# An attention block with a token mixer: the second column pair's fill goes first, and the last token pair takes narrow products over three steps

## The chip, the cores and the metric

The kernel runs on one core of a Trainium2 chip. The metric is device time in microseconds (us) of one execution. Below, PE is the matrix engine (TensorE) and PEld its weight loads, DVE is VectorE, ACT is ScalarE, POOL is GpSimd, and SP is SyncE, which issues most of the transfers (DMA).

## The reference, cut to what matters

Two residual blocks follow each other, on x with 2048 tokens and 512 channels, in float32:

```
h  = x + A(layernorm(x))      # linear attention, 32 heads of 16, dual softmax features, then @ wo
h2 = h + B(layernorm(h))      # token mixing:
    u = gelu(einsum("bsd,sf->bdf", hn, w1) + b1)     # contracts the 2048 tokens, F = 1792
    y = einsum("bdf,fs->bds", u, w2) + b2            # back to 2048 tokens
```

A needs all tokens' keys and values before any token's query can be finished. B's first product contracts the tokens, so it can start on the first tokens of h while the later ones are still in the attention.

## The kernel before, in words

**Precision.** Each float32 matrix product is made of three passes on rounded parts: high times high, high times low, low times high (`mm3`, lines 63 to 67). For every operand ACT writes the rounded part (`hi`), and DVE or POOL subtracts it from the source (`lo`; `split`, lines 58 to 61).

**Stages.** The 2048 tokens are 16 tiles of 128 (NT = 16). First come keys, values and some of the queries. Then the attention loop (lines 646 to 698) runs NT + 3 iterations; iteration `it` works on several tiles at once, each at another step: queries' features scaled on POOL (`s_pq`, line 463, and `s_ez`, line 445), transposes on PE (`s_tr`, line 530, copied out by ACT in line 532 as `pht`), numerators on PE (`s_num`, line 549, on every second iteration), the output projection (`s_wo`), the residual on DVE (`s_h`, line 577), and the second layernorm: `s_moments` on ACT, `s_rstd` on POOL (lines 588 and 589, tiles `r` and `ve`), and `s_hn` (line 593 on ACT, then the split: line 60 on ACT, line 61 on POOL). The result of `s_hn` is `HN[t]`, named `hs` in the profile.

**Fills.** B's first product is done in seven column pairs p of 256 columns of w1; each pair has two PSUM banks, `PU[p]` (named `pu`). `fill(p)` adds the share of one token tile to pair p: two `mm3`, so six matmuls of 128x512, shown at lines 65 to 67. In the attention loop `fills(it)` (lines 640 to 644) adds one tile to pair 0 and one to pair 1: pair 0 takes tile `it - 5`, pair 1 is a tile behind and takes tile `it - 6`. What is left of the pairs 0 and 1, and the pairs 2 to 6, runs after the loop, in an order that a scheduler makes. Weights come by DMA (line 611, `wraw`), ACT makes `whi` (line 612), DVE makes `wlo` (line 604). Within the attention loop the order on PE, DVE, ACT and POOL is that of the program text.

**Second product.** The outputs are made for pairs of token tiles, `sp` = 0 to 7. The two halves of F and the two tiles of a pair form a 2 by 2 block product, done by a scheme with seven products in place of eight, for each of seven steps p (`STEPS`, line 764). ACT and DVE prepare w2's sums in groups of two steps (`sums_w2`, `hi_w2` in line 793, `lo_w2` in line 802). The low parts live in two buffers, so a group's low part is written once the products of the group two before it are done.

**Wide and narrow products** (`product`, lines 818 to 825). A bank holds two halves of 256 columns. A wide product multiplies the high weights with both parts of `u` at once, 512 columns (line 820): high times high goes to half 0, high times low to half 1; then low times high, 256 columns, is added to half 0 (line 821). The two halves must be added on DVE later. A narrow product is three matmuls of 256 columns into one half (line 824), and needs no adding. In `PROD`, five of the seven products are wide; in `LAST`, for the last token pair, four are wide.

**Order at a pair's end.** The steps p = 0 to 4 run step by step (all seven products of a step). The last two steps run by product: product 0 of steps 5 and 6, then product 1 of both, and so on (line 857), so that the banks are complete one after another. For the last token pair the tail (lines 891 to 912) adds banks to the residual on DVE and writes three pieces of the output: one of 256 KB and two of 128 KB, the last at line 912.

Of the kernel before, what the change touches and what calls it, by code (L numbers as in the profile page):

```python
# [17 lines left out]
P = 128  # L18
S, D, H, DH, F = 2048, 512, 32, 16, 1792
NT = S // P  # L20
KD = D // P
NF = F // P
NP = NF // 2
HD = D // 2
# [6 lines left out]
LAG = 5  # L31
# [5 lines left out]
def block_kernel(ctx: ExitStack, tc: tile.TileContext, x, xT, wT, phic, wo, w1, b1, w2, b2,  # L37
                 kvmask, ident_in, out):
    nc = tc.nc
# [23 lines left out]
    def mm3(o, ah, al, bh, bl, first, last):  # L63

        nc.tensor.matmul(o, ah, bh, start=first, stop=False)  # L65
        nc.tensor.matmul(o, ah, bl, start=False, stop=False)  # L66
        nc.tensor.matmul(o, al, bh, start=False, stop=last)  # L67
# [3 lines left out]
    ps_q = ctx.enter_context(tc.tile_pool(name="ps_q", bufs=2, space=PSUM, side="right"))  # L71
# [290 lines left out]
    q = {"mm": 0, "logits": 0, "exp": 0, "sum": 0}  # L362
# [238 lines left out]
    def flush():  # L601
        while LATER:
            wl_, raw, wh_ = LATER.pop(0)
            LO.append(nc.vector.tensor_sub(wl_, raw, wh_).ins)  # L604
# [13 lines left out]
    FN, FL = [0] * (NF // 2), [0] * (NF // 2)  # L618

    def fill_load(p):  # L620
        if FL[p] < NT:
            WI[p, FL[p]] = stream(w1v, FL[p], 2, p * 256, 256)
            FL[p] += 2

    def fill(p, pool=None):

        t = FN[p]
        FN[p] = t + 1
        if FL[p] <= t:
            fill_load(p)  # L630
        if any(part is WI[p, t - t % 2][1] for part, _, _ in LATER):
            flush()
        if t == 0:
            PU[p] = [pool.tile([P, D], F32, name="pu", tag="pu") for _ in range(2)]
        a, b = WI[p, t - t % 2]
        for c in range(2):
            mm3(PU[p][c], a[:, t % 2, c * P:(c + 1) * P], b[:, t % 2, c * P:(c + 1) * P],
                HN[t][:, 0], HN[t][:, 1], t == 0, t == NT - 1)

    def fills(it):  # L640
        if FN[0] <= it - LAG:
            fill(0, ps_f)
        if FN[1] < it - LAG:
            fill(1, ps_q)

    for it in range(NT + 3):
        even = it % 2 == 0
# [23 lines left out]
        negate()  # L671
        q_mm()
        fills(it)
        q_exp(0)
        logits = q_logits(1)
# [110 lines left out]
    def hi_w2():  # L786

        g = done["hi"]
        if g == NGR:
            return  # L790
        done["hi"] += 1
        WH[g] = ws.tile([P, 7, GRP * P], F32R, name="whi", bufs=3)
        nc.scalar.activation(WH[g], RAW[g], AF.Copy)  # L793

    def lo_w2():

        g = done["lo"]
        if g == NGR:
            return
        done["lo"] += 1  # L800
        wl_ = ws.tile([P, 7, GRP * P], F32R, name="wlo", bufs=2)
        nc.vector.tensor_sub(wl_, RAW[g], WH[g])  # L802
        for i, step in enumerate(STEPS[g * GRP:(g + 1) * GRP]):
            AW[step] = WH[g][:, :, i * P:(i + 1) * P], wl_[:, :, i * P:(i + 1) * P]

    with tc.issue_after(LO[-18]), tc.issue_after(LD[-20]):
        for i in range(3):
# [5 lines left out]

    PROD = ((2, 1, 0, None), (5, 5, 1, None), (0, 0, 2, 0), (1, 4, 2, 1), (3, 6, 3, None), (6, 2, 4, None),
            (4, 3, 5, None))
    LAST = PROD[:-1] + ((4, 3, 5, 0),)

    def product(o, half, a, b, first, start, stop):
        if half is None:
            nc.tensor.matmul(o, a[0], b, start=start, stop=stop, skip_group_check=True)  # L820
            nc.tensor.matmul(o[:, 0], a[1], b[:, 0], start=False, stop=stop, skip_group_check=True)  # L821
            return
        for i, (x, y) in enumerate(((0, 0), (0, 1), (1, 0))):
            nc.tensor.matmul(o[:, half], a[x], b[:, y], start=start and first and i == 0, stop=stop and i == 2,  # L824
                             skip_group_check=True)

    def products(sp, ps, order):
        for a, b, bk, half in order:
            for p in ps:
                wh_, wl_ = AW[sp, p]  # L830
                product(bank[bk], half, (wh_[:, a], wl_[:, a]), UB[p, b], half != 1, p == 0, p == NP - 1)

    def flat(a):
        return a.rearrange("p k d -> p (k d)")
# [3 lines left out]
    for n, (sp, p) in enumerate(STEPS):  # L838
        t = 2 * sp
        last = t + 2 == NT  # L840
        if n % GRP == 0 and p < NP - 1:
            lo_w2()
            hi_w2()
            sums_w2()
        if p == 0:
            bank = []
            for _ in range(6):
                pool = (ps_f, ps_q, ps_b, ps_b)[n_bank % 8 // 2]
                bank.append(pool.tile([P, 2, HD], F32, name="py", tag="pu"))
                n_bank += 1  # L850
        order = LAST if last else PROD
        if p < NP - 2:
            products(sp, [p], order)
            continue
        if p < NP - 1:
            continue
        products(sp, [p - 1, p], order)
        e = uo.tile([P, 2, HD], F32, name="e")
        u2 = uo.tile([P, HD], F32, name="u2", bufs=1)
        u3 = uo.tile([P, HD], F32, name="u3")  # L860
        if not last:
            ot = uo.tile([P, 2, 2, HD], F32, name="ot", bufs=1)
            low = uo.tile([P, 3, HD], F32, name="low", bufs=1)
            nc.scalar.activation(e[:, 1], bank[0][:, 0], AF.Copy)
            for i in range(3):
                nc.scalar.activation(low[:, i], bank[3 + i][:, 1], AF.Copy)
            nc.vector.tensor_add(e[:, 1], bank[0][:, 1], e[:, 1])
            nc.vector.tensor_sub(u2, bank[1][:, 0], e[:, 1])
            nc.vector.tensor_add(u2, bank[1][:, 1], u2)
            nc.vector.tensor_sub(u3, u2, bank[2][:, 0])  # L870
            nc.vector.scalar_tensor_tensor(e[:, 0], bank[2][:, 1], -1.0, u2, op0=ALU.mult, op1=ALU.subtract)

            def out_block(i, h, o, add):
                nc.vector.scalar_tensor_tensor(ot[:, i, h], o, b2s[:, t + i:t + i + 1], add, op0=ALU.add, op1=ALU.add)  # L874

            out_block(0, 0, bank[2][:, 1], u3)
            out_block(0, 1, bank[3][:, 0], u3)
            nc.gpsimd.dma_start(out[t * P:(t + 1) * P, :], flat(ot[:, 0]), accum_op=ALU.add)  # L878
            if n % GRP == 0:
                lo_w2()  # L880
                hi_w2()
            out_block(1, 0, bank[4][:, 0], e[:, 0])
            out_block(1, 1, bank[5][:, 0], e[:, 1])
            nc.gpsimd.dma_start(out[(t + 1) * P:(t + 2) * P, :], flat(ot[:, 1]), accum_op=ALU.add)
            nc.gpsimd.dma_start(out[t * P:(t + 1) * P, HD:D], low[:, 0], accum_op=ALU.add)
            nc.gpsimd.dma_start(out[(t + 1) * P:(t + 2) * P, :], flat(low[:, 1:3]), accum_op=ALU.add)
            if n % GRP == 0:
                sums_w2()
            continue

        hb = [hp.tile([P, 2, HD], F32, name=f"hb{i}") for i in range(2)]
        for i in range(2):
            nc.sync.dma_start(flat(hb[i]), out[(t + i) * P:(t + i + 1) * P, :])
            nc.vector.tensor_scalar(hb[i], hb[i], b2s[:, t + i:t + i + 1], None, op0=ALU.add)
        nc.scalar.activation(e[:, 1], bank[0][:, 0], AF.Copy)
        nc.vector.tensor_add(e[:, 1], bank[0][:, 1], e[:, 1])
        nc.vector.tensor_add(hb[1][:, 1], e[:, 1], hb[1][:, 1])
        nc.vector.tensor_sub(u2, bank[1][:, 0], e[:, 1])
        nc.vector.tensor_add(u2, bank[1][:, 1], u2)
        nc.vector.tensor_sub(hb[1][:, 0], hb[1][:, 0], u2)  # L900
        nc.vector.tensor_sub(u3, u2, bank[2][:, 0])
        nc.vector.tensor_sub(hb[1][:, 0], hb[1][:, 0], bank[2][:, 1])
        nc.vector.tensor_add(hb[0], hb[0], u3.unsqueeze(1).to_broadcast([P, 2, HD]))
        nc.vector.tensor_add(hb[0][:, 0], bank[2][:, 1], hb[0][:, 0])
        nc.vector.tensor_add(hb[0][:, 1], bank[3][:, 0], hb[0][:, 1])
        nc.vector.tensor_add(hb[0][:, 1], bank[3][:, 1], hb[0][:, 1])
        nc.sync.dma_start(out[t * P:(t + 1) * P, :], flat(hb[0]))
        nc.vector.tensor_add(hb[1][:, 0], bank[4][:, 0], hb[1][:, 0])
        nc.vector.tensor_add(hb[1][:, 0], bank[4][:, 1], hb[1][:, 0])
        nc.scalar.dma_start(out[(t + 1) * P:NT * P, 0:HD], hb[1][:, 0])  # L910
        nc.vector.tensor_add(hb[1][:, 1], bank[5][:, 0], hb[1][:, 1])
        nc.sync.dma_start(out[(t + 1) * P:NT * P, HD:D], hb[1][:, 1])


def _layout(A_x, A_wqkv, A_w_phi, A_wo, B_w1, B_b1, B_w2, B_b2):
# [46 lines left out]
```

## Time and profile before

| | |
|---|---|
| median of 3 runs | 529.30 us (529.26 to 529.55) |
| the profiled execution | 529.31 us |
| its span, first to last instruction | 527.5 us |
| PE busy | 516.5 us (98%), 3343 matmuls |
| DVE, ACT, POOL busy | 394.5, 278.3, 246.6 us |
| granted PE clock, mean | 0.999 |

The span stands 1.8 us below the profiled execution's time; the rest lies around it. A PE matmul is shown as busy until its modelled end, and matmuls overlap, so busy time of PE hides short stops: these are read from the waits and from the distance of starts in the timeline. In a timeline row the first number is the start in us, the second the duration; "x8" is eight instructions merged in a row; in brackets stands how long the engine was idle before, and what ended the wait. The chain of waits goes back from the last instruction to what released it, and so on.

### The profile page before, as it was taken

Reading aid. Unit: us, or ns where it says so; the run is one execution under the profiler, and the core shown is the slowest. Engines: PE = TensorE matmul, PEld = TensorE weight load, DVE = VectorE, ACT = ScalarE, POOL = GpSimd, SP = SyncE. Lnnn points to the kernel's source line nnn. Section 1 sums busy time; section 2 is a strip of 40 time slices with the busy share of each in tenths; the row PEclk is TensorE's granted clock in tenths of the full one; section 3 lists DMA queues with packets and bytes.
Section 4 is the critical chain, followed back from the end, with each engine's and each line's share of the span. In section 5 each row is a group of like instructions: output and inputs, shape, how many; then the busy total and the mean of one; then the engine's idle time right before and its main releaser. Section 6 shows DMA issues by size and latency. Waiting matters only on the chain.

```text
span 527.5 us, 8840 instructions
## 1 busy us (share of the span) xinstructions
PE 516.5 (98%) x3343; PEld 434.1 (82%) x3343; DVE 394.5 (75%) x684; ACT 278.3 (53%) x481; POOL 246.6 (47%) x204
## 2 busy tenths in 40 slices
PE   8999999999999989999999999999999999999996
PEld 7888888887877767777788888888899999999995
DVE  6993999976899989875325523725779888988985
ACT  6999843534247776557746423625453434434430
POOL 2589699985999988887326000000002112111210
PEclk9999999999999999999999999999999999999999
DMA  8743310030122233334234354532215687668742
GB/s 298 203 129 121 84 39 21 1 86 18 49 93 80 91 96 115 109 111 139 85 99 119 99 161 155 166 98 80 69 51 113 160 187 169 135 146 198 141 61 60
DMA packets 36298, 58.52 MB, mean 111 GB/s; under 512 B 3744, under 2 KB 19360, under 8 KB 36256
## 3 DMA queue, kind: packets, MB, share of 16 engines
q1 hardware_dynamic: 31936, 51.37, 31.2%
q0 software_dynamic: 4032, 6.42, 9.6%
q8 instruction: 26, 0.43, 0.4%
q10 hardware_dynamic: 288, 0.17, 0.1%
q14 instruction: 16, 0.13, 0.1%
HBM read 46.81 MB, written 11.14 MB: 110 GB/s over the span
## 4 chain that ended last, share of the span: by engine, by line
PE 80%; POOL 12%; DVE 4%; ACT 2%; DMA 1%; issue 0%; DVEq 0%; POOLq 0%; ACTq 0%
PE py L820 12%; PE pu L65 11%; PE pu L66 10%; PE pu L67 10%; PE py L824 8%; PE py L821 6%; POOL ez L445 4%; POOL eq L463 3%; PE pv L66 3%; PE pv L67 3%; PE pv L65 3%; PE pk_ps L65 2%; PE pk_ps L67 2%; PE pk_ps L66 2%; POOL hs L61 2%; PE kvp L210 2%
## 5 line engine op out<-in xcount | busy, mean ns | idle before, releaser
L604 DVE TENSOR_TENSOR wlo<-wraw,whi 128x512 fp32r<-128x512 f32 x56 | 50.6, 908 | 54.6 <-ACT whi L612 53.4
L66 PE MATMUL pu<-hs,whi 128*128 128x512 f32 x224 | 87.6, 391 | 2.1 <-POOL hs L61 2.1
L65 PE MATMUL pu<-hs,whi 128*128 128x512 f32 x224 | 87.5, 395 | 0.0
L67 PE MATMUL pu<-hs,wlo 128*128 128x512 f32 x224 | 87.3, 390 | 0.0
L878 POOL DMA_DIRECT2D out<-ot x7 | 6.2, 889 | 149.1 <-DVE ot L874 149.1
L793 ACT ACTIVATE whi<-wraw 128x1792 fp32r<-128x1792 f32 x28 | 47.4, 1701 | 46.7 <-PE py L820 20.6
L820 PE MATMUL py<-uf,whi 128*128 128x512 f32 x195 | 70.9, 399 | 0.0
L802 DVE TENSOR_TENSOR wlo<-wraw,whi 128x1792 fp32r<-128x1792 f32 x28 | 56.5, 2022 | 12.0 <-PE py L821 8.9
L612 ACT ACTIVATE whi<-wraw 128x512 fp32r<-128x512 f32 x56 | 34.9, 626 | 47.3 <-PE pu L66 43.0
L821 PE MATMUL py<-uf,wlo 128*128 128x256 f32 x195 | 54.9, 282 | 0.0
L66 PEld LDWEIGHTS pu<-hs,whi 128*128 128x128 f32 x224 | 42.1, 188 | 11.5 <-POOL hs L61 3.1
L65 PEld LDWEIGHTS pu<-hs,whi 128*128 128x128 f32 x224 | 42.1, 188 | 10.8 <-issue 2.5
L67 PEld LDWEIGHTS pu<-hs,wlo 128*128 128x128 f32 x224 | 42.1, 188 | 9.0 <-DVE wlo L604 0.4
L820 PEld LDWEIGHTS py<-uf,whi 128*128 128x128 f32 x195 | 36.8, 189 | 7.3
L445 POOL TENSOR_TENSOR ez<-eq,zB 128x1024 f32<-128x1024 f32 x16 | 40.6, 2539 | 4.4 <-ACT zB L492 4.4
L821 PEld LDWEIGHTS py<-uf,wlo 128*128 128x128 f32 x195 | 36.9, 189 | 0.0
L198 POOL TENSOR_TENSOR pk<-pk,sk 128x1024 f32<-128x1024 f32 x16 | 31.0, 1943 | 7.9 <-DVE sk L197 5.3
L463 POOL TENSOR_TENSOR eq<-eq,w 128x1024 f32<-128x1024 f32 x16 | 31.9, 1997 | 1.2 <-DVE w L460 1.2
L824 PE MATMUL py<-uf,whi 128*128 128x256 f32 x170 | 32.0, 283 | 0.0
L202 POOL TENSOR_TENSOR zacc<-zacc,pk 128x1024 f32<-128x1024 f32 x13 | 31.2, 2402 | 0.5
L61 POOL TENSOR_TENSOR hs<-hn,hs 128x512 fp32r<-128x512 f32 x16 | 21.4, 1337 | 17.8 <-ACT hs L60 17.8
L820 PE MATMUL py<-un,whi 128*128 128x512 f32 x78 | 28.8, 399 | 0.0
(183 smaller groups left out, 1317.8 us busy)
## 6 DMA issues: line engine op xcount, KB each, us to landing
wraw<-in_w SPq DMA_DIRECT2D x56, 256.0 KB, 2.8
wraw<-in_w SPq DMA_DIRECT2D x28, 512.0 KB, 4.4
xraw<-in_xT SPq DMA_DIRECT2D x16, 256.0 KB, 2.9
xh<-in_x SPq DMA_DIRECT2D x16, 256.0 KB, 2.7
h<-in_x SPq DMA_DIRECT2D x16, 256.0 KB, 3.0
out<-h SPq DMA_DIRECT2D x16, 256.0 KB, 3.0
out<-ot POOLq DMA_DIRECT2D x14, 256.0 KB, 4.5
wraw<-in_wT SPq DMA_DIRECT2D x12, 256.0 KB, 5.2
```

The source lines that it names most:

```text
L65: nc.tensor.matmul(o, ah, bh, start=first, stop=False)
L66: nc.tensor.matmul(o, ah, bl, start=False, stop=False)
L67: nc.tensor.matmul(o, al, bh, start=False, stop=last)
L445: nc.gpsimd.tensor_mul(EZ[t], EQ[t], zB)
L463: nc.gpsimd.tensor_mul(heads(EQ[t]), heads(EQ[t]), W[t].rearrange("p g c h -> p (g c h)").unsqueeze(2).to_broadcast([P, 2 * H, DH]))
L604: LO.append(nc.vector.tensor_sub(wl_, raw, wh_).ins)
L612: nc.scalar.activation(wh_, raw, AF.Copy)
L793: nc.scalar.activation(WH[g], RAW[g], AF.Copy)
L802: nc.vector.tensor_sub(wl_, RAW[g], WH[g])
L820: nc.tensor.matmul(o, a[0], b, start=start, stop=stop, skip_group_check=True)
L821: nc.tensor.matmul(o[:, 0], a[1], b[:, 0], start=False, stop=stop, skip_group_check=True)
L824: nc.tensor.matmul(o[:, half], a[x], b[:, y], start=start and first and i == 0, stop=stop and i == 2, skip_group_check=True)
```

## The change

Two edits. In the attention loop, `fills` does pair 1 ahead of pair 0; no other order of the loop changes. For the last token pair, all seven products become narrow, so that four banks are used in place of six and the tail's additions of two halves go away (10 additions and subtractions on DVE in place of 14, the two of b2 counted in neither); and the last three steps (4, 5 and 6) run by product, in place of the last two.

```
     def fills(it):
+        if FN[1] < it - LAG:
+            fill(1, ps_q)
         if FN[0] <= it - LAG:
             fill(0, ps_f)
-        if FN[1] < it - LAG:
-            fill(1, ps_q)
...
-    LAST = PROD[:-1] + ((4, 3, 5, 0),)
+    LAST = ((2, 1, 0, 0), (5, 5, 0, 1), (0, 0, 1, 0), (1, 4, 1, 1), (3, 6, 2, 0), (6, 2, 2, 1), (4, 3, 3, 0))
...
-        if p < NP - 2:
+        run_on = 3 if last else 2
+        if p < NP - run_on:
             products(sp, [p], order)
             continue
         if p < NP - 1:
             continue
-        products(sp, [p - 1, p], order)
+        products(sp, range(NP - run_on, NP), order)
...
         nc.scalar.activation(e[:, 1], bank[0][:, 0], AF.Copy)
-        nc.vector.tensor_add(e[:, 1], bank[0][:, 1], e[:, 1])
-        nc.vector.tensor_add(hb[1][:, 1], e[:, 1], hb[1][:, 1])
-        nc.vector.tensor_sub(u2, bank[1][:, 0], e[:, 1])
-        nc.vector.tensor_add(u2, bank[1][:, 1], u2)
+        nc.vector.tensor_add(hb[1][:, 1], bank[0][:, 0], hb[1][:, 1])
+        nc.vector.tensor_sub(u2, bank[0][:, 1], e[:, 1])
         nc.vector.tensor_sub(hb[1][:, 0], hb[1][:, 0], u2)
-        nc.vector.tensor_sub(u3, u2, bank[2][:, 0])
-        nc.vector.tensor_sub(hb[1][:, 0], hb[1][:, 0], bank[2][:, 1])
+        nc.vector.tensor_sub(u3, u2, bank[1][:, 0])
         nc.vector.tensor_add(hb[0], hb[0], u3.unsqueeze(1).to_broadcast([P, 2, HD]))
-        nc.vector.tensor_add(hb[0][:, 0], bank[2][:, 1], hb[0][:, 0])
-        nc.vector.tensor_add(hb[0][:, 1], bank[3][:, 0], hb[0][:, 1])
-        nc.vector.tensor_add(hb[0][:, 1], bank[3][:, 1], hb[0][:, 1])
+        nc.vector.tensor_add(hb[0][:, 0], bank[1][:, 1], hb[0][:, 0])
+        nc.vector.tensor_sub(hb[1][:, 0], hb[1][:, 0], bank[1][:, 1])
+        nc.vector.tensor_add(hb[0][:, 1], bank[2][:, 0], hb[0][:, 1])
         nc.sync.dma_start(out[t * P:(t + 1) * P, :], flat(hb[0]))
-        nc.vector.tensor_add(hb[1][:, 0], bank[4][:, 0], hb[1][:, 0])
-        nc.vector.tensor_add(hb[1][:, 0], bank[4][:, 1], hb[1][:, 0])
-        nc.scalar.dma_start(out[(t + 1) * P:NT * P, 0:HD], hb[1][:, 0])
-        nc.vector.tensor_add(hb[1][:, 1], bank[5][:, 0], hb[1][:, 1])
-        nc.sync.dma_start(out[(t + 1) * P:NT * P, HD:D], hb[1][:, 1])
+        for k, o, q in ((0, bank[2][:, 1], nc.scalar), (1, bank[3][:, 0], nc.sync)):
+            nc.vector.tensor_add(hb[1][:, k], o, hb[1][:, k])
+            q.dma_start(out[(t + 1) * P:NT * P, k * HD:(k + 1) * HD], hb[1][:, k])
```

## The prediction

> **What bounds the kernel now.** I read the page's shares first, then busy time by stretch, then the waits, then the chain.
>
> ```profile
> span 527.5 us, 8840 instructions
> PE 80%; POOL 12%; DVE 4%; ACT 2%; DMA 1%; issue 0%; DVEq 0%; POOLq 0%; ACTq 0%
> ```
>
> The profiled execution took 529.31 us, 0.01 above the median of the runs, so 1.8 us lie around the span; the sum below is made against 529.31. Four fifths of the chain that ends last is PE. An eighth is POOL, and I want to know where that lies.
>
> ```profile
> 185.00:240.00 55.00, 51.12 (x358) 39.41 (x356) 47.54 (x87) 35.37 (x76) 48.08 (x37) 1.00 0.35 106
> 240.00:505.00 265.00, 265.00 (x1457) 228.50 (x1450) 174.60 (x285) 124.01 (x193) 45.27 (x52) 1.00 0.50 128
> ```
>
> The columns are PE, PEld, DVE, ACT, POOL busy, the clock, DMA. From 240 to 505 PE is never idle. From 185 to 240, the later part of the attention loop, it misses 3.9 us, and POOL works 48 of 55.
>
> ```profile
> ACT hn L593 <- POOL ve L589: 23.6, 13, 3.3
> ...
> POOL hs L61 <- ACT hs L60: 17.8, 10, 3.1
> ...
> PE pu L66 <- POOL hs L61: 2.1, 3, 1.0
> PE tn L549 <- ACT pht L532: 1.6, 2, 1.4
> ```
>
> These are whole waits in us, how often, and the longest. PE stops for two things: for `hs`, the layernormed tile that pair 0's fill needs (the first edit's target), and for `pht` ahead of `s_num`. Which of the two sets the end is read from the chain, here its last POOL piece:
>
> ```profile
> 229.31 1.89 POOL eq L463
> 231.21 1.23 POOL hs L61
> 232.43 2.81 POOL ez L445
> 235.24 0.51 POOL r L588
> 236.05 0.83 ACT hn L593
> 236.90 0.63 ACT hs L60
> 237.53 0.53 ACT whi L612
> 238.06 0.97 ACT pht L532 x2
> 239.08 1.10 PE tn L549 x32
> ```
>
> POOL's queue runs without a hole up to the reciprocal root `r` and `ve`; ACT, waiting for them, makes `hn` and `hs`, and behind these in its queue stands `pht`, for which PE's `s_num` waits. No PE instruction is in this chain. From 239.08 on it is PE, up to the tail.
>
> The tail, from the chain again:
>
> ```profile
> 518.55 0.39 ACT e L895
> 518.97 0.43 DVE e L896
> ...
> 521.44 0.33 DVE hb L902
> 521.77 0.61 DVE hb L903
> ```
>
> and as a timeline, then the last transfer in the view of DMA issues (its 1.7 us is from issue to landing):
>
> ```profile
> 518.23 0.28 PE L821 MATMUL py<-uf,wlo 128*128 128x256 f32 x1
> ...
> 522.51 0.28 PE L824 MATMUL py<-uf,wlo 128*128 128x256 f32 x1
> ...
> 524.33 0.41 DVE L911 TENSOR_TENSOR hb<-py,hb 128x256 f32<-128x256 f32 x1
> ...
> 524.77 0.34 SPq L912 DMA_DIRECT2D out<-hb  x1
> ```
>
> ```profile
> out<-hb SPq DMA_DIRECT2D x1, 128.0 KB, 1.7
> ```
>
> The last matmul ends at 522.51 + 0.28 = 522.79. DVE is in one unbroken run of 14 additions from 518.97 on and ends at 524.33 + 0.41 = 524.74, 1.95 us after PE. So here DVE is the bound.
>
> **First edit: pair 1's fill ahead of pair 0's.** It adds and removes nothing; six matmuls of 128x512 change places with six. Pair 1 uses a tile that is one iteration older, so its six can run while POOL makes `hs`. Stops for `hs`, 2.1 us by the waits, should go. What is late next is `s_num`: in the chain above it starts when `pht` is there, and that hangs on POOL and ACT alone. Each us that PE is earlier it waits more at line 549. The iterations before 185 have no such stop, and from 239.08 on PE has the same work to do. So I cost the edit at 0. The cover is POOL's chain; were it gone, up to 2.1 us would be gained, and this is the first rival. Can the block lose? Inside it, pair 1's operands must be ready 6 matmuls earlier; after it, everything stands where it stood on PE. No other engine's waits change in the built program: POOL, DVE and SP have the same order and wait for the same producers, and ACT has one `whi` behind instead of ahead of a short `ve` late in the loop, where the chain is PE's:
>
> ```profile
> 267.50 0.28 ACT L585 ACTIVATE ve<-ve,eps 128x1 f32<-128x1 f32 x1
> ```
>
> I take 0, since the chain is the nearest row; as bounds I keep -2.1 and, for that `ve` should its `whi` be wanted at once, +0.3.
>
> **Second edit, the matmuls.** Four wide products in each of seven steps become narrow: 28 times, two matmuls (512 and 256 columns) become three of 256. The columns streamed are the same 768. From the timeline:
>
> ```profile
> 503.05 0.41 PE L820 MATMUL py<-uf,whi 128*128 128x512 f32 x1
> ...
> 505.17 0.40 PE L820 MATMUL py<-un,whi 128*128 128x512 f32 x1
> ...
> 519.05 0.41 PE L824 MATMUL py<-uf,whi 128*128 128x256 f32 x2
> ...
> 520.49 0.40 PE L820 MATMUL py<-uf,whi 128*128 128x512 f32 x1
> ```
>
> Between the first two starts lie six wide products: 2.12 / 6 = 0.353 each. Between the other two, four narrow ones: 1.44 / 4 = 0.360. So PE's end moves by 28 x 0.007 = 0.2 us. This is the first term, +0.2.
>
> The Trainium skill, page "TensorE: Matmul & The Clock Gate", section "Back-to-back issue gap", lets a warm matmul of 256 columns take 262 cycles and one of 512 take 518, at 2.4 GHz. By it, an estimate, a narrow product takes 786 cycles and a wide one 780, 2.5 ns apart, so 28 of them make 0.07 us and the whole sum would be -1.4. The trace has longer spacings than that page for both, 0.360 and 0.353.
>
> **Second edit, the order.** Steps 4, 5 and 6 by product: 21 products of 0.36. Groups of three end 1.08 us apart. Readers in the built program wait for a whole bank. So bank 0 (products 0 and 1) is full 15 products before PE's end, 5.4 us; bank 1 3.2 us before; bank 2 1.1 us before; bank 3 at the end. The additions take 0.33 to 0.43 in the chain, the wide one 0.61:
> - after bank 0: ACT's copy 0.39 and three additions, 1.6 us with the steps between engines: done 3.8 before the end;
> - after bank 1: 0.6 + three of 0.4 = 1.8: done 1.4 before;
> - after bank 2: two, 0.8: done 0.3 before;
> - after bank 3: one, 0.42.
>
> DVE is never behind, so its end is PE's end + 0.04 (as from the bank's last matmul, ending 518.51, to the copy at 518.55) + 0.42 = PE's end + 0.46, in place of + 1.95. Second term: -1.49. The transfer behind it is the same 128 KB on the same queue, with the two others issued farther ahead of it; I leave its 1.7 and what follows as they are.
>
> One thing the new order needs earlier: the low weights of steps 5 and 6, by the third matmul of step 5's product 0.
>
> ```profile
> 512.93 2.02 DVE L802 TENSOR_TENSOR wlo<-wraw,whi 128x1792 fp32r<-128x1792 f32 x1 [1.64 <-PE py L824]
> 515.15 0.39 PE L820 MATMUL py<-uf,whi 128*128 128x512 f32 x1
> ```
>
> DVE makes them from 512.93 to 514.95, after PE has freed their buffer (end of step 2). Step 4 starts at 515.15; the third matmul of the second product comes 0.36 + 2 x 0.12 later, 515.75. That leaves 0.8 us; a wait here costs what it exceeds that.
>
> **Sum.** 0 + 0.2 - 1.49 = -1.3: 529.31 - 1.3 = 528.0 us, 0.25% less.
>
> **Rivals.**
> 1. *PE's stops for `hs` are on the path.* Then 2.1 us go too: 525.9 (the starts under rival 2 show 1.6 for the first stop, where the waits show 1.0, so it could be 3). For it: they are PE's only stops besides `pht`. Against: the chain above, and ACT's 23.6 us of waits for POOL's `ve`.
> 2. *One long stop lowers the clock.* The fills of the first stopped iteration, twelve matmuls from line 65 up to line 530, and the stop behind them:
>
> ```profile
> 185.39 0.47 PE L65 MATMUL pu<-hs,whi 128*128 128x512 f32 x1
> ...
> 189.79 1.03 PE L530 MATMUL tn<-ident,eq 128*128 128x128 f32 x8
> ...
> 194.98 0.45 PE L549 MATMUL tn<-pht,kvB 64*32 64x256 f32 x8 [1.42 <-ACT pht L532]
> ```
>
> ```profile
> 526.00:527.00 1.00, 0.00 (x0) 0.00 (x0) 0.00 (x0) 0.00 (x0) 0.00 (x0) 0.71 0.06 18
> ```
>
>    They take 4.40; at 0.353 for 768 columns (above), twelve of 512 would take 2.8. So PE comes 1.6 earlier to line 549 and stops for 1.42 + 1.6 = 3.0 us at a stretch. The second row is a stretch after PE's end: the clock is 0.71 in the mean of 526 to 527, so, if it went to half, it did so near 526.4, 3.6 us after the last matmul. Against: 3.0 is less than 3.6, though that is one sample. At half speed for as long as that, PE would lose 1.8; the other stops up to 239 (3.7 of all waits less the longest, 1.0 and 1.4) take 1.3 of it. Time: 528.0 + 0.5 = 528.5. The Trainium skill, same page, section "Part 1: The HAM clock gate (the "warmup" mystery)", has the clock halved after an idle window of about 3.4 us; 3.0 stays below that as well.
> 3. *Slower: narrow matmuls run at the pace of their weight loads.* Each has its own.
>
> ```profile
> L824 PEld LDWEIGHTS py<-uf,whi 128*128 128x128 f32 x170 | 26.2, 189 | 1.8
> ```
>
>    The last pair becomes one unbroken run of 49 narrow products, 147 matmuls. If each took a load's 0.189 in place of 0.12, that is 49 x 0.21 = 10.3 more: 538.3. It eats the gain from a spacing of 0.13 on (147 x 0.009 = 1.3). Against: the twelve in a row above at 0.12 each, with the loads overlapping.
> 4. *The tail doesn't follow PE*: the low weights come late by most of a further `L802` (2.02 less 0.8 = 1.2), or the landing doesn't move with its issue. Then the gain shrinks to 0.1 to 0.9: about 528.8.
>
> **Chances.** Forecast 0.74, rival 1 0.08, rival 2 0.04, rival 3 0.03, rival 4 0.11. 0.2%, 1.06 us, is about what a measurement of this kernel can tell from no change. The forecast's gain of 1.3 may be 1.0 to 1.6 (0.2 more or less on matmuls, the same on the last landing), so I give 0.64 of its 0.74 to faster; with rival 1 that is 0.72. Same: the other 0.10, rivals 2 and 4, so 0.25. Slower: 0.03. The range runs from 527.0 (the forecast's best, 527.7, and a third of rival 1's 2.1) to 528.9 (rival 4); rival 1 in full and rival 3 are outside, 0.11.
>
> **What would show it.** After: the wait of line 66 for `hs` gone, the wait of line 549 for `pht` grown by as much, 1.6 to about 3.7, with line 549 of the same iterations starting at 194.98 and 239.08 as before; if these starts come earlier, rival 1 holds. The last matmul near 523.0, then one DVE addition, the last issue near 523.5, a span near 526.2. A gap on PE for `wlo` near 515.7 would be rival 4; a spacing over 0.12 in the last 17 us rival 3; a granted clock under 1 after 195 rival 2.

## The result and the profile after

The changed kernel takes 528.31 us (median of 20 executions, 527.80 to 529.31), the kernel before beside it 529.68 (20 executions, 529.23 to 530.17). The ratio is 0.9975, with a 95% interval of 0.9969 to 0.9982: 0.25% faster, 1.37 us. The forecast was 1.3 less, 528.0 from a profiled execution of 529.31; both forms of it are met.

The profiled execution of after took 528.52 us, so again 1.8 lie around its span. Its page and its busy time by stretch:

```profile
span 526.7 us, 8893 instructions
PE 81%; POOL 12%; DVE 3%; ACT 2%; issue 0%; POOLq 0%; ACTq 0%
```

```profile
185.00:240.00 55.00, 50.37 (x346) 39.52 (x352) 47.54 (x87) 35.34 (x76) 48.08 (x37) 1.00 0.35 109
240.00:505.00 265.00, 265.00 (x1478) 228.12 (x1460) 175.26 (x285) 124.44 (x194) 44.38 (x52) 1.00 0.49 128
```

POOL still has its 12% of the chain and its 48.08 us between 185 and 240. Before the two traces are compared, one offset must be taken out. The same early matmuls, from the chain of before and then from that of after:

```profile
9.92 3.02 PE pk_ps L127 x12
```

```profile
10.43 3.03 PE pk_ps L127 x12
```

After is 0.51 us late within its first 10 us, where both kernels do the same work. That is scatter between executions, so 0.5 has to be subtracted from every later start of after. Now PE's waits of after, and the end of the piece of its chain that the prediction quoted:

```profile
PE tn L549 <- ACT pht L532: 3.8, 2, 2.8
...
PE po L65 <- DVE h L577: 0.8, 1, 0.8
```

```profile
235.81 0.51 POOL r L588
...
236.61 0.82 ACT hn L593
...
237.46 0.63 ACT hs L60
238.09 0.52 ACT whi L612
238.61 0.98 ACT pht L532 x2
...
239.63 1.10 PE tn L549 x32
```

The wait at line 66 for `hs` is gone, the one at line 549 for `pht` has grown from 1.6 to 3.8, and `s_num` starts at 239.63 in place of 239.08: at the same time, once the offset is taken out. PE reaches the same door earlier and stands longer in front of it. The tail, as a timeline:

```profile
518.17 0.38 ACT L896 ACTIVATE e<-py 128x256 f32<-128x256 f32 x1 [6.39 <-PE py L824]
...
520.33 0.42 DVE L900 TENSOR_TENSOR u<-u,py 128x256 f32<-128x256 f32 x1 [0.53 <-PE py L824]
...
522.49 0.42 DVE L904 TENSOR_TENSOR hb<-py,hb 128x256 f32<-128x256 f32 x1 [0.23 <-PE py L824]
...
523.25 0.28 PE L824 MATMUL py<-uf,wlo 128*128 128x256 f32 x1
...
523.57 0.42 DVE L907 TENSOR_TENSOR hb<-py,hb 128x256 f32<-128x256 f32 x1 [0.32 <-PE py L824]
...
524.02 0.34 SPq L908 DMA_DIRECT2D out<-hb  x1
```

DVE now waits for PE in front of each bank (the brackets at lines 900, 904 and 907). PE ends at 523.25 + 0.28 = 523.53, DVE at 523.57 + 0.42 = 523.99: 0.46 behind it in place of 1.95.

### The profile page after: what moved, and what is told of

Same layout as the page of the kernel before. It is cut to its first block, busy times and chain, and to the rows that moved or that the text cites. A ratio compares the mean times of both kernels' runs of the same rounds, so it can differ in the third digit from the quotient of the medians.

```text
span 526.7 us, 8893 instructions
## 1 busy us (share of the span) xinstructions
PE 517.0 (98%) x3371; PEld 436.3 (83%) x3371; DVE 394.0 (75%) x680; ACT 278.5 (53%) x481; POOL 245.2 (47%) x204
## 4 chain that ended last, share of the span: by engine, by line
PE 81%; POOL 12%; DVE 3%; ACT 2%; issue 0%; POOLq 0%; ACTq 0%
PE py L820 11%; PE pu L65 11%; PE pu L66 10%; PE pu L67 10%; PE py L824 10%; PE py L821 6%; POOL ez L445 4%; POOL eq L463 3%; PE pv L66 3%; PE pv L67 3%; PE pv L65 3%; PE pk_ps L65 2%; PE pk_ps L67 2%; PE pk_ps L66 2%; POOL hs L61 2%; PE kvp L210 2%
## 5 line engine op out<-in xcount | busy, mean ns | idle before, releaser
L820 PE MATMUL py<-uf,whi 128*128 128x512 f32 x175 | 63.4, 399 | 0.0
L821 PE MATMUL py<-uf,wlo 128*128 128x256 f32 x175 | 49.2, 281 | 0.0
L824 PE MATMUL py<-uf,whi 128*128 128x256 f32 x210 | 39.0, 283 | 0.0
L820 PEld LDWEIGHTS py<-uf,whi 128*128 128x128 f32 x175 | 33.0, 188 | 6.8
L824 PEld LDWEIGHTS py<-uf,whi 128*128 128x128 f32 x210 | 32.4, 189 | 1.4
L821 PEld LDWEIGHTS py<-uf,wlo 128*128 128x128 f32 x175 | 33.1, 189 | 0.0
```

## The experiments

Theory: the gain is the tail's alone, and of the tail its order; the first edit gains nothing because POOL's chain sets the time at which the attention loop ends. Rivals: PE's stops for `hs` were on the path; the gain comes from the shorter list of additions; a stop of 2.8 us lowers PE's clock. Differences in us below are against the kernel before beside the experiment on the same chip, or, where the text says so, against after. The time of after, 528.31 us, was taken beside other executions of the kernel before (529.68); beside the experiments that kernel took 529.71 to 529.86, so a difference against after can be off by up to 0.2 us.

### Each edit alone

`e1_fills`: the kernel before with the first edit only.

```
     def fills(it):
+        if FN[1] < it - LAG:
+            fill(1, ps_q)
         if FN[0] <= it - LAG:
             fill(0, ps_f)
-        if FN[1] < it - LAG:
-            fill(1, ps_q)
```

> The kernel before with the first edit alone (pair 1's fill ahead of pair 0's). Forecast: no change, within 0.2 us of the kernel before (529.7), PE's wait at line 66 for hs gone, its wait at line 549 for pht 3.5 to 3.8 us in place of 1.6. Rival 1 (the stops for hs are on the path): about 2.1 us less, 527.6. A third reading, that the 1.4 us of the whole change come in equal parts from both edits: 0.7 us less.

Measured: 529.89 against 529.71, ratio 1.0002 (0.9993 to 1.0011). PE's waits: 3.5 us for `pht`, none for `hs`. So the stops are gone and nothing is gained; rival 1, and an equal share of both edits, are out.

`e2_tail`: the kernel before with the second edit only (its lines are those of the change).

> The kernel before with the second edit alone (narrow products in the last pair, its last three steps by product, the shorter list of additions). Forecast: the whole gain, 1.3 to 1.4 us less, about 528.3; DVE's last addition ends 0.46 us after PE's last matmul in place of 1.95. If the first edit had a part in the gain, this is 0.7 us less or nearer to the kernel before.

Measured: 528.26 against 529.71, ratio 0.9974 (0.9964 to 0.9984): the whole gain. DVE ends 0.46 us behind PE.

### What in the tail gains

`e3_order`: the kernel before with three steps by product, nothing else.

```
-        if p < NP - 2:
+        run_on = 3 if last else 2
+        if p < NP - run_on:
             products(sp, [p], order)
...
-        products(sp, [p - 1, p], order)
+        products(sp, range(NP - run_on, NP), order)
```

> The kernel before with its last three steps by product in place of two, and nothing else: the wide products, the six banks and the 14 additions stay. Theory (what counts is how long before PE's end each bank is full): bank 0 is full 18 products of 0.353 = 6.4 us before PE's end, bank 1 5.3, bank 2 3.2, bank 3 2.1, bank 4 1.1; with additions of 0.4 (the wide one 0.61) DVE is done with bank 3 0.5 us before PE's end, with bank 4 0.3 behind it and with bank 5 0.7 behind it, in place of 1.95. So 1.25 us less, and nearly the whole gain without narrow products. Rival (the gain is in the shorter list of additions): under 0.6 us less.

`e4_narrow2`: the second edit with two steps by product in place of three.

```
-        run_on = 3 if last else 2
+        run_on = 2
```

> The second edit alone, but with the last two steps by product in place of three: narrow products, four banks, the shorter list of additions. Theory: groups of two products end 0.72 us apart; bank 0 is full 3.6 us before PE's end, bank 1 2.2, bank 2 0.7, so DVE is done with them 2.0 and 0.2 before and 0.6 behind PE's end, and ends 1.0 us behind it in place of 1.95. With 0.2 for the narrow matmuls 0.75 us less than the kernel before. Rival (the shorter list alone does it): 1.3 us less, as with three steps.

What the timelines show of the ends, and the times:

| kernel | PE ends | DVE ends | DVE behind PE | expected | time | ratio (95%) |
|---|---|---|---|---|---|---|
| before | 522.79 | 524.74 | 1.95 | | 529.71 | |
| e2_tail: three steps, 10 additions | 523.55 | 524.01 | 0.46 | 0.46 | 528.26 | 0.9974 (0.9964 to 0.9984) |
| e3_order: three steps, 14 additions | 523.75 | 524.31 | 0.56 | 0.7 | 528.03 | 0.9967 (0.9955 to 0.9979) |
| e4_narrow2: two steps, 10 additions | 523.38 | 524.29 | 0.91 | 1.0 | 529.12 | 0.9987 (0.9979 to 0.9996) |

Two timelines show why. In e3_order, with all its 14 additions, DVE still gets a pause in front of bank 2:

```profile
519.50 0.42 DVE L901 TENSOR_TENSOR hb<-hb,u 128x256 f32<-128x256 f32 x1
520.59 0.42 DVE L902 TENSOR_TENSOR u<-u,py 128x256 f32<-128x256 f32 x1 [0.67 <-PE py L824]
...
523.90 0.41 DVE L912 TENSOR_TENSOR hb<-py,hb 128x256 f32<-128x256 f32 x1
```

In e4_narrow2, with 10, the first can start only at 520.23, and from there on there is none:

```profile
520.23 0.42 DVE L897 TENSOR_TENSOR hb<-py,hb 128x256 f32<-128x256 f32 x1 [4.00 <-ACT e L896]
...
523.54 0.75 DVE L907 TENSOR_TENSOR hb<-py,hb 128x256 f32<-128x256 f32 x2
```

The order over three steps takes away 1.39 of the 1.49 us by itself, without a single narrow product or a shorter list; the shorter list by itself takes away 1.04. The order suffices, and it costs PE nothing. The shorter list does not: the narrow products that come with it cost PE 0.2, and e4_narrow2 gains 0.6 in time (0.75 expected), where e3_order gains 1.7 (1.25 expected) and e2_tail 1.45. With these 0.2 added to DVE's lag, the times stand in the order of the lags; but e3_order and e2_tail, 0.23 apart, can't be told from each other by their intervals.

### What hides the first edit

`e8_load`: after, with POOL's reciprocal root made twice.

```
+        for _ in range(2):
             nc.gpsimd.tensor_tensor(r2[:, t:t + 1], VE[t][:, 0:1], mhalf[:, :1], op=ALU.pow)
```

> The changed kernel with POOL's reciprocal root (line 588, 0.5 us) made twice for each token tile, the same value. Theory (POOL's chain sets the pace from about 165 or 185 to 240, some 10 tiles): each repeat in that stretch counts in full, 10 x 0.5 = 5 us more, and PE's stops at line 549 grow by as much in sum. Rival (PE's own order sets the pace): under 1 us more. Besides, the stops of PE get longer than the 2.8 us of the changed kernel; if the granted clock falls below 1 behind one of over 3.6 us, the limit lies between.

Measured: 534.55, 6.2 more than after; ratio to before 1.0092 (1.0078 to 1.0107). POOL's groups between 165.16 and 245, and PE's first and last start of line 549 there:

```profile
L589 POOL TENSOR_TENSOR r<-ve,mhalf 128x1 f32<-128x1 f32 x20 | 12.4, 619 | 1.4 <-ACT ve L585 0.7
```

```profile
165.16 1.09 PE L549 MATMUL tn<-pht,kvB 64*32 64x256 f32 x32
...
245.35 1.10 PE L549 MATMUL tn<-pht,kvB 64*32 64x256 f32 x32 [1.66 <-ACT pht L532]
```

There are 20 roots in place of 10, 619 ns each: 6.2 us more POOL work. The stretch from the first of these starts to the last is 80.19 us; in after, whose first start follows, it is 239.63 - 165.71 = 73.92.

```profile
165.71 1.09 PE L549 MATMUL tn<-pht,kvB 64*32 64x256 f32 x32
```

The difference is 6.27. What POOL gets more to do is added in full, although PE and ACT have idle time there. That is what "POOL's chain sets the pace" means, and it is now measured and not only read from a chain. Two points of the expectation failed. A root took 0.62 us in the mean and not 0.5, so 6.2 us came and not 5. And PE's stops at line 549 grew from 3.8 to 7.0 us in sum, by 3.2 and not by as much as the time: for 6.7 us the clock was at half (shown at the end), PE worked for 5.75 of them, and so needed some 2.9 us more for the same work. The repeat lengthens both POOL's queue and the path from `ve` to `hs`, so this run alone does not tell which of the two counts; the next one leaves POOL's work as it is and only fills its queue.

`e7_hole`: after, with POOL's holes filled. In the timeline of after, POOL stands idle once in two iterations, between its root and the split that ACT prepares from it:

```profile
206.22 0.19 POOL L589 TENSOR_TENSOR ve<-ve,r 128x1 f32<-128x1 f32 x1
208.01 1.29 POOL L61 TENSOR_TENSOR hs<-hn,hs 128x512 fp32r<-128x512 f32 x1 [1.59 <-ACT hs L60]
209.27 1.93 POOL L463 TENSOR_TENSOR eq<-eq,w 128x1024 f32<-128x1024 f32 x1
```

The edit makes `hn` and `hs` of the odd tiles in the next iteration, behind `eq`:

```
         if it > 1 and even:
             if it <= NT:
                 s_num(it // 2 - 1)
-            if it >= 4:
-                s_hn(it - 4)
+        if it >= 4:
+            s_hn(it - 4)
...
-        if it >= 3 and even:
+        if it == NT + 2:
             s_hn(it - 3)
```

> The changed kernel, with hn, hs of the odd token tiles made in the next iteration, behind POOL's eq (line 463) in place of ahead of it, as for the even tiles. POOL's work is the same; the hole of 1.6 us in its queue, in which it waits for ACT's hn and hs in each second iteration, is filled by eq. Theory: five such holes lie between 185 and 240, 8 us, more than PE's 3.8 us of stops, so the time falls by 2.5 to 3.8 us below the changed kernel, to 525. Rival (what PE waits for, pht, hangs on ACT's own queue and not on POOL): no change.

`e10_hole_oldfills`: the same with the fills in their old order.

> As e7_hole, but with the fills in their old order. Here POOL's chain is 8 us shorter, so what the order of the fills is worth can show. Theory: with the chain out of the way PE is the bound, and what PE stops for counts; pair 0's operand hs now comes one eq (1.9 us) later, so in the old order PE stops for it and the kernel is 0.5 to 2 us slower than e7_hole (526.3 to 527.8). Rival (hs is ready in time all the same): within 0.3 us of e7_hole.

Measured: e7_hole 525.77, ratio to before 0.9927 (0.9915 to 0.9938), 2.5 us less than after. e10_hole_oldfills 524.93, ratio 0.9906 (0.9891 to 0.9922): the fastest kernel of this study, and 0.8 faster than with the new order of fills. The two ran on different chips, five and four times; their times do not overlap (525.65 to 526.13, 524.26 to 525.04), the intervals of their ratios do by a little. So the theory on e7_hole holds, at the low end of what it expected, and my expectation for e10_hole_oldfills had the wrong sign. The stretch of line 549 agrees; its first and last start in e7_hole, then in e10_hole_oldfills:

```profile
165.53 1.09 PE L549 MATMUL tn<-pht,kvB 64*32 64x256 f32 x32
...
237.21 1.09 PE L549 MATMUL tn<-pht,kvB 64*32 64x256 f32 x32
```

```profile
165.71 1.09 PE L549 MATMUL tn<-pht,kvB 64*32 64x256 f32 x32
...
236.04 1.09 PE L549 MATMUL tn<-pht,kvB 64*32 64x256 f32 x32
```

These are 71.68 and 70.33 us, against 73.92 in after. POOL's work is the same; its waits for `hs` from 165 to 240 are 1.2 us in both, in place of 6.6 in after (for `ve` at its root they grow from 0.7 to 2.4 and 2.0). So its holes are what counted. Between the two orders of the fills the stretch differs by 1.35 us. PE's waits, e7_hole first:

```profile
PE tn L549 <- ACT pht L532: 1.6, 1, 1.6
PE pu L67 <- DVE wlo L604: 1.2, 1, 1.2
```

```profile
PE pu L66 <- POOL hs L61: 0.7, 1, 0.7
PE tn L549 <- ACT pht L532: 0.4, 1, 0.4
```

The old order stops 0.7 for `hs`. The new order stops 1.2 for `wlo`: DVE's two subtractions of the low weights, in the timelines of e7_hole and then e10_hole_oldfills, stand at the same place,

```profile
192.81 4.07 DVE L604 TENSOR_TENSOR wlo<-wraw,whi 128x512 fp32r<-128x512 f32 x2
```

```profile
192.96 4.11 DVE L604 TENSOR_TENSOR wlo<-wraw,whi 128x512 fp32r<-128x512 f32 x2
```

but pair 1's fill, which needs what they write, comes first on PE in e7_hole and waits:

```profile
196.94 0.50 PE L67 MATMUL pu<-hs,wlo 128*128 128x512 f32 x1 [1.17 <-DVE wlo L604]
```

With pair 0 ahead of it there is no such stop. The stop of 1.6 for `pht` in e7_hole costs nothing; the starts of line 549 on both sides of the stop for `wlo` show it, e7_hole first:

```profile
194.01 1.10 PE L549 MATMUL tn<-pht,kvB 64*32 64x256 f32 x32 [1.64 <-ACT pht L532]
...
209.38 1.09 PE L549 MATMUL tn<-pht,kvB 64*32 64x256 f32 x32
```

```profile
194.15 1.10 PE L549 MATMUL tn<-pht,kvB 64*32 64x256 f32 x32 [0.37 <-ACT pht L532]
...
208.21 1.09 PE L549 MATMUL tn<-pht,kvB 64*32 64x256 f32 x32
```

Counted from the first start in each kernel, the upper rows lie at 28.48 and 28.44 us: up to there the order of the fills changes nothing, as behind POOL's chain in after. The lower rows lie at 43.85 and 42.50, and the whole 1.35 us has come in between, where the stop of 1.17 for `wlo` is (the other 0.2 is not traced further). So where POOL's chain sets the pace the first edit is worth nothing, and where it no longer does the edit loses.

`e5_relief`: after, with the low part of `hs` made by DVE for the odd tiles. `e6_relief_oldfills`: the same with the old order of fills.

```
-        split(HN[t][:, 0], HN[t][:, 1], hn, nc.gpsimd)
+        split(HN[t][:, 0], HN[t][:, 1], hn, nc.vector if t % 2 else nc.gpsimd)
```

> The changed kernel, with the low part of hs (line 61, 1.27 us on POOL and in each second iteration 1.6 us of POOL idle ahead of it) made by DVE for the odd token tiles. Theory (POOL's chain sets the pace from 185 to 240, PE's 3.8 us of stops at line 549 are all that it holds back): POOL gets 2.9 us per two iterations, so those stops go and the time falls by 2.5 to 3.8 us below the changed kernel, to 525. Rival (the stretch is bound by something else, PE's own order or DVE): no change, or slower by what DVE's added 8 x 0.7 us delays.

> As e5_relief, but with the fills in their old order (so the second edit and the relief of POOL). Theory: with POOL no longer the bound, the stops for hs go with those for pht, so this is within 0.5 us of e5_relief. If the order of the fills is worth something as soon as POOL's chain is out of the way: up to 2.1 us slower than e5_relief.

Measured: e5_relief 527.33, ratio 0.9953 (0.9941 to 0.9965), only 1.0 less than after in place of 2.5 to 3.8. PE's waits for `pht` went from 3.8 to 0.4 us, but DVE's own work became late:

```profile
PE pu L65 <- DVE eq L148: 1.3, 1, 1.3
...
PE pu L67 <- DVE wlo L604: 1.0, 1, 1.0
...
PE po L65 <- DVE h L577: 0.5, 1, 0.5
```

The work was moved to the engine that was next in line (DVE is busy for 47.54 of the 55 us above). Here filling POOL's hole gained more than moving work off POOL.

e6_relief_oldfills gave two groups: five executions at 526.8 to 527.0, seven at 530.5 to 532.0, the latter with a mean granted clock of 0.993 to 0.994. Over all twelve the ratio to before is 0.9988 (0.9967 to 1.0009), no difference that can be told. In the faster group it stands 0.4 below e5_relief, as expected; its slower group was not expected. Two more profiles were taken to see where the clock falls:

> A second look at the kernel of e6_relief_oldfills, whose executions fell in two groups, five at 526.8 to 527.0 with a mean granted clock of 0.999 and seven at 530.5 to 532.0 with 0.993 to 0.994; the profile at hand is of the first group. Theory: in the second group the granted clock goes to half behind PE's stop of 1.8 us (line 65, waiting for DVE's h), for some 7 us, and as POOL is relieved there is no slack after it, so that half of them are lost. If this look falls in the first group it tells nothing; if it falls in the second and the clock falls somewhere else, the theory is wrong.

> A third look at the kernel of e6_relief_oldfills; the two so far fell in its faster group. As before: in the slower group the granted clock should be at half for about 7 us behind PE's stop of 1.8 us at line 65, and the 3.6 us should be lost between there and the end of the attention loop, since no slack follows. In the faster group it tells nothing.

Both fell in the faster group (526.7, clock 0.999). So where its clock falls, and why the same kernel with the new order of fills had no such group in five executions, stays open.

`e9_hole_order3`: e7_hole with the tail of e3_order.

> The two parts that the runs so far point to, together: hn and hs of the odd token tiles made in the next iteration behind POOL's eq, with the new order of fills (as in e7_hole), and the tail of e3_order (wide products, six banks, 14 additions, three steps by product). e7_hole gave 525.8 with the narrow products, e3_order was 0.2 us faster than e2_tail. Theory (the two lie in different stretches and add): 525.6, within 0.2. Rival (the difference of e3_order and e2_tail was scatter between executions): 525.8 or a little more.

Measured: 525.95 (525.61 to 526.72), ratio 0.9933 (0.9920 to 0.9946); e7_hole had 525.65 to 526.13. That is above the 525.4 to 525.8 expected, so no further gain is seen; what 0.2 us the wide products might give is below what these few executions tell apart. This kernel has the new order of fills and ran on the chip of e10_hole_oldfills: it stops there for `wlo` for 1.17 us as e7_hole does, and takes 1.0 more than e10_hole_oldfills.

### The clock behind one long stop

In the profile of after the clock stays at 1.00 after PE's stop of 2.8 us. In the profile of e1_fills, with the same stop (2.76), it does not:

```profile
196.08 1.10 PE L549 MATMUL tn<-pht,kvB 64*32 64x256 f32 x32 [2.76 <-ACT pht L532]
```

```profile
194.00:197.50 3.50, 1.42 (x34) 0.85 (x35) 3.50 (x3) 3.44 (x9) 3.50 (x3) 1.00 0.43 130
197.50:201.00 3.50, 3.50 (x10) 2.73 (x9) 2.51 (x5) 2.02 (x4) 3.42 (x4) 0.51 0.45 150
201.00:204.00 3.00, 3.00 (x14) 2.49 (x14) 2.79 (x9) 1.92 (x6) 3.00 (x3) 1.00 0.29 87
```

For some 3.4 us the clock is at half, from 1.4 us after PE has begun to work again. That takes 1.7 off PE, or 0.003 of the mean clock. Of the 20 executions of after, eleven have a mean clock of 0.997 and eight one of 0.999 or 1.0. The eleven took 527.8 to 528.5 us, the eight 528.1 to 528.9: the fall of the clock shows no cost. (The mean clock alone does not say where a fall lies. That it comes with the first edit is borne out by e2_tail, the same kernel with the old order of fills: 0.999 or 1.0 in all eight executions. But beside these nine of 25 executions of the kernel before, its longest, have 0.997 or 0.998 too, and none of them was traced.) The reason is the same chain; line 549's first and last start in e1_fills, then its first in the kernel before:

```profile
166.29 1.09 PE L549 MATMUL tn<-pht,kvB 64*32 64x256 f32 x32
...
240.20 1.10 PE L549 MATMUL tn<-pht,kvB 64*32 64x256 f32 x32 [0.71 <-ACT pht L532]
```

```profile
165.20 1.09 PE L549 MATMUL tn<-pht,kvB 64*32 64x256 f32 x32
```

From first to last it is 73.91 us with the clock at half in between, and 239.08 - 165.20 = 73.88 before. Only PE's slack was used; its later stop for `pht` is 0.71 us, 1.05 in after. The one execution left, at 0.992, took 529.31, the longest.

The Trainium skill, page "TensorE: Matmul & The Clock Gate", section "Part 1: The HAM clock gate (the "warmup" mystery)", has the clock halved after at least one idle window of about 3.4 us, in windows that run freely. The 3.4 us of half clock and the chance from one execution to the next agree with such windows. A whole window without work was not needed here: a stop of 2.76 us was enough, and the measurement decides. What counts as work is not shown: the stop ends with 32 matmuls on weights of only 64x32, and the clock fell 4.2 us after the stop began (197.5 less 193.3).

## Why the prediction was right, point by point

- **First edit, 0.** Right, with its reason: the stops for `hs` became a longer wait at line 549 (3.8 us; about 3.7 forecast), and its starts at 194.98 and 239.08 moved by the offset alone (195.51, 239.63). e1_fills measures 0.1 (ratio 0.9993 to 1.0011, -0.4 to +0.6 us), e8_load the cover, 6.27 us for 6.2 us of POOL work. The stated price of the lost cover, up to 2.1 us gained, did not come: with POOL's holes filled the old order stops only 0.7 us for `hs`, and the new order costs 0.8. The sentence "pair 1's operands must be ready 6 matmuls earlier" named the place, but I gave it no price; it is the stop of 1.2 us for `wlo`.
- One wait was not foreseen: 0.76 us on PE for DVE's `h` (line 577). It lies ahead of the last wait for `pht` and so costs nothing.
- **Second edit, matmuls, +0.2.** Right. The last pair's first row in the timeline of after is

```profile
505.73 0.40 PE L824 MATMUL py<-un,whi 128*128 128x256 f32 x2
```

  and PE ends at 523.53: 17.80 us, against 505.17 to 522.79 before: 17.62. That is 0.18 more for 28 conversions. The issue gaps on the Trainium skill's page, named in the prediction, would give 0.07; this trace gives more.
- **Second edit, order, -1.49.** Right to the hundredth: 0.46 in place of 1.95. The additions came as forecast, with a wait in front of each bank, and no stop for `wlo` near 515.7. What the prediction did not separate is that the order alone gives nearly all of it (e3_order).
- **Sum, -1.3.** 0.18 - 1.49 = -1.31 on the trace; the spans differ by 526.7 - 527.5 = -0.8, and the 0.5 of a later start is to be added to that. The runs measure -1.37.
- **Rival 2.** Its mechanism, to which I gave 0.04, is seen in the profile of e1_fills (a stop of 2.76; 3.0 forecast) and, as far as the mean clock tells, came in about half of the executions of after. Its price, 0.5, was the step of this rival that failed: it set only 1.3 us of slack against the lost PE time. In after the stops behind the long one are 0.76 + 1.05 = 1.81 us, and e1_fills, with 1.7 us lost, still stops for 0.71 at the end. The loss falls into the slack that POOL's chain leaves, the same cover that hides the first edit.
- **Rivals 1, 3 and 4** did not come: no earlier start at line 549 (e1_fills), narrow matmuls at 17.80 / 147 = 0.121 us each, and a last landing of 1.7 us as before.

## What to carry to other kernels

A stop of PE that vanishes is worth nothing until the next thing that PE waits for comes earlier as well; follow that one back, and test it by giving its engine a little more work: if the time grows by the whole of it, look there for holes before you touch the order on PE. At a kernel's end, count how long before the last matmul each bank is complete: completing banks earlier, by the order of the same products, hides the additions without making them fewer. An edit that is neutral behind another engine's chain can lose as soon as that chain is shortened (here 0.8 us), so it should be weighed again then.

## What the runs showed of the hardware

- The granted clock went to half for 3.4 us, from 1.4 us behind a PE stop of 2.76 us (e1_fills); in the profile of after, with a stop of 2.77, it stayed at 1.00. In e8_load it was at half for 6.7 us, and that began within a stop of 3.22 us, some 0.9 us before its end at 197.45:

```profile
196.50:203.20 6.70, 5.75 (x41) 3.76 (x42) 5.26 (x7) 4.62 (x11) 6.54 (x6) 0.50 0.38 120
```

- POOL's reciprocal root on 128x1 elements takes 619 ns in the mean, though the multiplication behind it on the same shape takes 0.19 us (206.22 in the timeline of after). It counts in full on POOL's chain: ten more of them lengthened it by 6.27 us.
- The start of an execution differs by up to 1.1 us between executions: line 549's first start lies at 165.16 in e8_load and 166.29 in e1_fills, with the same work before it. That is as much as most single times of one kernel scatter.
